# Multiplying w_in by g on two engines instead of three, and storing the remainder rows 64 at a time

## The chip, the core and the metric

The kernel runs on one core of a Trainium2 chip. The metric is the device time of one execution in microseconds; the median of three executions stands for the kernel. The profile is of one further execution, whose own time is given beside its span below. Engine names are those of the profile: PE is TensorE, PEld its weight load, DVE is VectorE, ACT is ScalarE, POOL is GpSimd, SP is SyncE.

## The reference

An attention without softmax, an RMS norm over each head, and a two-layer network with a sigmoid gate, in float32:

```python
# q, k, v: (8, 8, 576, 64); g_norm: (64,); w_in: (512, 2048); w_out: (2048, 512)
kv = np.einsum('bhsd,bhse->bhde', k, v)
out = np.einsum('bhsd,bhde->bhse', q, kv)
rms = np.sqrt(np.mean(out * out, axis=-1, keepdims=True) + 1e-06)
attn_out = out / rms * g_norm
x = attn_out.transpose(0, 2, 1, 3).reshape(B * S, H * D)      # 4608 x 512
h = x @ w_in
g = h * (1.0 / (1.0 + np.exp(-1.702 * h)))
result = g @ w_out                                             # 4608 x 512
```

## The kernel before

**Tiles and passes.** The kernel works in fp16 with float32 sums and has nine passes of the network, `dense(t, ...)`, t = 0 to 8, over 512 rows each. Passes 0 to 7 take the first 512 of the 576 rows of batch t. The 64 rows that each batch has left over are collected in `x_rem` (8 times 64 is 512) and are pass 8. The attention of batch t+1 is woven into pass t as small units that two dictionaries place by hand: `at1(i, f)` runs f after the i-th column block of the first product, `at2(n, f)` after the n-th matmul of the second. The schedule is manual: instructions stand on each engine in the order in which the code emits them, and semaphores are put in where one engine uses what another has made.

**One pass.** The first product (L440) multiplies `w_in_sb`, cut into four blocks `ko` of 128 rows and 2048 columns, by the transposed activations; ScalarE applies the gate (L449) and writes `gT`. The second product (L549), in the class `Seven` (passes 1 to 8), needs seven block products instead of eight, in `ORDER = (1, 5, 6, 2, 7, 3, 4)`, two row blocks `mo` of eight matmuls each, which is 112 matmuls. VectorE forms the sums `gS` (L481) and, from pass 1 on, the sums and copies into the output tile `osb` (L525, L528). In pass 1 the units for batch 2 are: `pack_k` (L227), `kv` (L236, into PSUM; `keep_kv`, L249, copies it to `kvb` in two halves on VectorE), `rows(j)` (L300, four matmuls that need `kvb`, placed at n = 1, 7, 14, 20), their squares on ScalarE (L308), `add_up` (L314), `roots` (L323, L324), `turn` (L327) with a DMA transpose (L333), and `out` for the remainder rows (L279). Pass 2 has the same units.

**w_in times g.** In pass 0 and pass 1 `g_norm` is applied to the activations (L358). From pass 2 on it is in the weights: during the second product of pass 1, which no longer reads `w_in_sb`, `scale_w_in(ko, engine)` multiplies the four blocks, 128x2048 each, in place by the column `g_col` (L206 on ScalarE, L208 on GpSimd or VectorE). Block 0 is on GpSimd at n = 0, block 1 on ScalarE at n = 48, blocks 2 and 3 on VectorE at n = 84 and 96. Pass 2 begins with `mm(ko, fo)` for ko = 0 to 3 on its first column block, so it needs all four within its first four matmuls. On VectorE the scalings stand among `apply` (L362) of the remainder rows of two batches (n = 74 and 80) and the sums L525 into `osb`.

**The last stores.** In pass 8 row block `mo` of `osb` holds the remainder rows of batches 2 mo and 2 mo + 1, 64 partitions each. `place` calls `store_rest` as soon as a quarter is ready: for (1, 1), the right halves of blocks 2 and 3, first; then (0, 1), which completes blocks 0 and 1; then (1, 0), the left halves of blocks 2 and 3. In `out` the rows of one batch's remainder are consecutive for batches from `EARLY` = 2 on; for batches 0 and 1 they are nine rows apart by a step in the index. For blocks with 2 mo >= 2, that is 1, 2 and 3, `store_rest` makes one transfer for both batches, shaped 2 x 64 x columns on the side of `out` and 128 partitions on the side of `osb` (L579); with two queues given it cuts the columns in half. Only block 0 is stored in two transfers of 64 rows (L585), one on SP and one on ScalarE. After the last store SP waits for every transfer to land (L845), and the program ends.

Of the kernel before, what the change touches and what calls it, by code (L numbers as in the profile page):

```python
# [16 lines left out]
def kernel(  # L17
# [10 lines left out]
    nc = tc.nc  # L28

    B, H, S, D = q.shape  # L30
    DM = H * D
# [5 lines left out]
    SM = 512  # L37
    J = SM // P
    R = S - SM
    assert R == 64 and B * R == SM and KO == NPAIR and 2 * D == P  # L40
    NT = B + 1
    EARLY = 2
    PE_ = 96
    NJ = S // PE_
# [36 lines left out]
    HF, HN = FO // 2, DM // 2  # L81
# [61 lines left out]
    for n in "kqv":  # L143
        if n != "q":
            rows = stage.tile([P, H, J * D], F32, name="qf", tag="qf")
            rows = rows.rearrange("p h x -> p (h x)")[0:PE_]
# [8 lines left out]
        out=ident,  # L155
        in_=ident,
# [303 lines left out]
    class Seven:  # L460
# [58 lines left out]
        def place(self, name, mo, with_, i, j):  # L519
            ps, m = self.ready(name, mo)  # L520
            if ps is None:
                return
            o = osbs[self.t][:, 2 * i + m.start : 2 * i + m.stop, j * HN : (j + 1) * HN]
            if with_:
                nc.vector.tensor_add(o, ps, self.kept[with_][:, m])  # L525
            else:
                copy = nc.vector.tensor_copy if self.t == B else nc.scalar.copy
                copy(o, ps)  # L528
            if self.t == B:
                if (i, j) == (1, 0):  # L530
                    store_rest(2 + mo, 0, HN, (nc.sync, nc.scalar))
                elif (i, j) == (1, 1):
                    store_rest(2 + mo, HN, DM, (nc.sync,))
                elif (i, j) == (0, 1):
                    store_rest(0, 0, DM, (nc.sync, nc.scalar))
                    store_rest(1, 0, DM, (nc.sync,))
            elif self.t in HALVED and j == 1 - i:
                store(self.t, 2 * i, 2 * i + 2)

# [31 lines left out]

    def store_rest(mo, n0, n1, queues):
        osb = osbs[B]
        if 2 * mo >= EARLY:
            rows = out.rearrange("(b s) n -> b s n", b=B)[2 * mo : 2 * mo + 2, SM:S, n0:n1]
            half = (n0 + n1) // 2
            parts = [(n0, n1)] if len(queues) == 1 else [(n0, half), (half, n1)]
            for queue, (a, b) in zip(queues, parts):
                queue.dma_start(out=rows[:, :, a - n0 : b - n0], in_=osb[:, mo, a:b])  # L579
            return  # L580
        for g in range(2):
            p0 = SM % PE_
            rows = out[(2 * mo + g) * S : (2 * mo + g + 1) * S, n0:n1]
            rows = rows[bass.DynSlice(NJ * p0 + SM // PE_, R, step=NJ), :]
            queues[g].dma_start(out=rows, in_=osb[g * R : (g + 1) * R, mo, n0:n1])  # L585

    def dense(t, units1, units2, group, deep, hid=None):
# [68 lines left out]
    def store(t, j0, j1):  # L656
        nc.sync.dma_start(
            out=out[t * S : t * S + SM, :].rearrange("(p j) m -> p j m", j=J)[:, j0:j1],
            in_=osbs[t][:, j0:j1],
        )  # L660
# [94 lines left out]
    for t in range(NT):  # L755
        b = t + 1
        u1, u2 = {}, {}

        def at1(i, f, *args):
            u1.setdefault(i, []).append(lambda: f(*args))  # L760

        def at2(i, f, *args):
            u2.setdefault(i, []).append(lambda: f(*args))  # L763

        def of(b, name, *args):
            return lambda: getattr(live[b], name)(*args)

        if t == 0:
            at1(7, of(0, "out", NPAIR))
            at2(4, setattr, a0, "ss_pool", Attention.ss_pool)  # L770
            at2(4, of(0, "ss", NPAIR, True))
            at2(4, of(0, "apply", NPAIR))
            at1(8, start, 1)
            for l in range(2):
                r = slice(l * PH, (l + 1) * PH)
                at1(8, nc.vector.memset, kpad[r, :, :, (1 - l) * D : (2 - l) * D], 0.0)
            for c in range(NPAIR):
                at1(12, of(1, "pack_q", c))
                at2(9 + 3 * c, of(1, "q", c))
                at2((21, 21, 38, 38)[c], of(1, "pack_k", c))  # L780
                at2((36, 37, 46, 47)[c], of(1, "kv", c))
                o = (41, 43, 52, 53)[c]
                at2(o, of(1, "out", c))
                if c == NPAIR - 1:
                    at2(48, load_kv, 2)
                at2((45, 48, 56, 58)[c], of(1, "ss", c))
                at2((48, 51, 56, 60)[c], of(1, "apply", c))
        elif b < B:
            if t == 1:
                at1(5, weight_sums)  # L790
                at2(64, setattr, live[1], "ss_pool", Attention.ss_pool)
                at2(64, of(1, "out", NPAIR))
                at2(80, of(1, "ss", NPAIR))
                at2(80, of(1, "apply", NPAIR))
                at2(0, scale_w_in, 0, nc.gpsimd)
                at2(48, scale_w_in, 1, nc.scalar)
                at2(84, scale_w_in, 2, nc.vector)
                at2(96, scale_w_in, 3, nc.vector)
            f0 = 5 if t == 1 else 2
            at1(f0, cast_q, b)  # L800
            at1(f0, start, b)
            at1(f0, of(b, "transpose_q"))
            if t + 2 < B:
                at1(12 if t == 1 else f0, load_q, t + 2)
                at1((11 if t == 1 else 9) + 4, load_kv, t + 2)
            for c in range(NPAIR):
                at1(f0, of(b, "pack_k", c))
                at1((11 if t == 1 else 9) + c, of(b, "kv", c))
            at2(21, nc.scalar.preload_act_table_set, "natural_log_exp_and_others")
            for j in range(J):  # L810
                at2((1, 7, 14, 20)[j], of(b, "rows", j))
                at2((5, 12, 18, 26)[j], of(b, "add_up", j))
                at2((33, 34, 35, 36)[j], of(b, "turn", j))
            at2(32, of(b, "roots"))
            at2(38, of(b, "out", NPAIR))
            at2(74, of(b, "ss", NPAIR))
            at2(74, of(b, "apply", NPAIR))
            at2(82, nc.scalar.preload_act_table_set, "gelu_apprx_sigmoid_and_others")
        dense(t, u1, u2, (GROUP, 5)[t] if t < 2 else 0, t == 0, None if t else d0)
# [30 lines left out]
```

## Time and profile before

| | us |
|---|---|
| median of three executions | 297.94 (296.08 to 298.21) |
| the profiled execution | 298.24 |
| its span, first to last instruction | 295.8 |

| engine | busy us | share of the span | instructions |
|---|---|---|---|
| PE | 269.0 | 91% | 2136 |
| ACT | 165.5 | 56% | 281 |
| DVE | 161.6 | 55% | 328 |
| POOL | 47.5 | 16% | 74 |

The mean granted clock of TensorE over the span is 0.966. The largest groups are the first product, L440 (512 matmuls with 128x512 outputs, 116.5 us), and the second, L549 (some 900 matmuls with 128x256 outputs). 36.70 MB are read from memory and 9.44 MB written. The profile cuts the span into 40 slices of 7.4 us and gives the busy share of each engine in tenths, the granted clock, and the mean share of the core's 16 DMA engines. Instruction rows are: start in us, duration in us, engine, line, operation, output<-inputs, and in brackets how long the engine had been idle and what released it.

### The profile page before, as it was taken

The numbers are of one execution on the slowest core, as the hardware profiler recorded it, in microseconds if no ns is written. First come the engines' busy times: TensorE is split into PE (matmuls) and PEld (weight loads), VectorE is DVE, ScalarE is ACT, GpSimd is POOL, SyncE is SP. The second block draws the span as 40 slices with busy tenths as digits, with TensorE's granted clock in tenths as the row PEclk, the third lists the DMA queues.
The fourth block names the chain that finished last, engine by engine and source line by source line (L and its number), as shares of the span: only waits on it lengthen the run. The fifth ranks groups of instructions, "written<-read, shape, count | busy, mean of one in ns | idle before, by whom it ended". The sixth has DMA issues, their size and how long they took to land.

```text
span 295.8 us, 5285 instructions
## 1 busy us (share of the span) xinstructions
PE 269.0 (91%) x2136; PEld 175.3 (59%) x2136; DVE 161.6 (55%) x328; ACT 165.5 (56%) x281; POOL 47.5 (16%) x74
## 2 busy tenths in 40 slices
PE   8899999947999999999999999999999999999600
PEld 5444544425864786578558845984697468548500
DVE  2640647996586578476756757684673342052300
ACT  2787258733876665676558475846675751573000
POOL 8852470073001101020111011000000000000000
PEclk9999999995999999999999999999999999999955
DMA  8999999796249957993897499457007000300211
GB/s 175 195 199 206 204 268 222 173 209 127 40 119 180 225 95 196 185 192 71 218 177 152 80 219 240 78 142 152 2 2 212 1 2 0 142 2 1 55 50 36
DMA packets 55400, 38.79 MB, mean 131 GB/s; under 512 B 31152, under 2 KB 52400, under 8 KB 55248
## 3 DMA queue, kind: packets, MB, share of 16 engines
q0 software_dynamic: 16016, 15.55, 33.0%
q1 hardware_dynamic: 39018, 22.65, 31.2%
q8 instruction: 16, 0.26, 0.4%
q10 hardware_dynamic: 342, 0.26, 0.3%
q14 instruction: 8, 0.07, 0.1%
HBM read 36.70 MB, written 9.44 MB: 156 GB/s over the span
## 4 chain that ended last, share of the span: by engine, by line
PE 71%; DMA 12%; DVE 8%; ACT 2%; issue 1%; POOL 0%; DVEq 0%
PE hT L440 33%; PE o L549 32%; DMA w_out_sb<-in_moe_w_out_dram 4%; DMA vbuf<-in_v_dram 4%; DVE gS L481 3%; PE kvp L236 2%; PE outR L300 2%; DMA kraw<-in_k_dram 2%; DMA qraw<-in_q_dram 2%; DVE kpad L227 1%; PE o L618 1%; DVE xT L358 1%; DVE x L327 1%; ACT ln L346 0%; DVE qbuf L136 0%
## 5 line engine op out<-in xcount | busy, mean ns | idle before, releaser
L440 PE MATMUL hT<-xT,w_in_sb 128*128 128x512 f16 x512 | 116.5, 379 | 0.1
L449 ACT ACTIVATE gT<-hT 128x512 f16<-128x512 f32 x144 | 84.5, 601 | 40.7 <-PE hT L440 40.6
L440 PEld LDWEIGHTS <-w_in_sb 128*128 128x128 f16 x576 | 54.5, 98 | 61.1 <-issue 0.6
L549 PEld LDWEIGHTS <-gS 128*128 128x128 f16 x512 | 49.7, 99 | 5.8
L481 DVE TENSOR_TENSOR gS<-gT 128x512 f16<-128x512 f16 (+1 forms) x48 | 24.5, 510 | 45.0 <-ACT gT L449 44.7
L549 PE MATMUL o<-tw,gS 128*128 128x256 f16 x384 | 47.7, 275 | 0.0
L549 PEld LDWEIGHTS <-gT 128*128 128x128 f16 x384 | 37.8, 100 | 6.2
L549 PE MATMUL o<-w_out_sb,gT 128*128 128x256 f16 x256 | 35.1, 281 | 0.0
L227 DVE COPY kpad<-kraw 64x576 f16<-64x576 f16 x56 | 25.0, 446 | 1.3
L525 DVE TENSOR_TENSOR osb<-o,s 128x512 f32<-128x512 f32 (+1 forms) x25 | 16.6, 664 | 15.2 <-issue 9.7
L112 POOL DMA_DIRECT2D kraw<-in_k_dram x16 | 9.9, 622 | 78.3 <-DVE kpad L227 56.9
L308 ACT ACTIVATE sq<-outR 128x512 f16<-128x512 f32 x24 | 14.4, 600 | 12.0 <-PE outR L300 12.0
L314 DVE TENSOR_REDUCE sum<-sq 128x8 f32<-128x512 f16 x24 | 16.4, 684 | 6.4 <-ACT sq L308 6.0
L327 DVE TENSOR_TENSOR x<-outR,sum 128x512 f16<-128x512 f32 x24 | 14.9, 683 | 6.2 <-ACT sum L324 6.2
L517 ACT COPY s<-o 128x512 f32<-128x512 f32 (+1 forms) x26 | 14.3, 550 | 6.5 <-PE o L549 6.4
L618 PE MATMUL o<-w_out_sb,gT 128*128 128x512 f16 x64 | 16.9, 379 | 0.1
L346 ACT ACTIVATE ln<-ss,eps_t 128x512 f32<-128x512 f32 (+1 forms) x16 | 9.3, 582 | 13.4 <-PE ss L344 13.2
L481 DVE TENSOR_TENSOR gS<-gS,gT 128x512 f16<-128x512 f16 (+1 forms) x24 | 16.2, 674 | 0.6
L763 ACT ACT_TABLE_LOAD x12 | 15.4, 1283 | 0.2
L300 PE MATMUL outR<-kvb,qTd 128*128 128x128 f16 x96 | 10.3, 232 | 5.7 <-DVE kvb L249 5.7
L549 PE MATMUL o<-w_out_sb,gS 128*128 128x256 f16 x128 | 15.4, 273 | 0.0
L549 PE MATMUL o<-tw,gT 128*128 128x256 f16 x128 | 15.3, 273 | 0.0
(77 smaller groups left out, 213.3 us busy)
## 6 DMA issues: line engine op xcount, KB each, us to landing
qf<-in_q_dram SPq DMA_DIRECT2D x5, 1024.0 KB
out_dram<-osb SPq DMA_DIRECT2D x10, 512.0 KB
kraw<-in_k_dram POOLq DMA_DIRECT2D x12, 288.0 KB, 7.4
vbuf<-in_v_dram POOLq DMA_DIRECT2D x12, 288.0 KB, 6.9
out_dram<-osb SPq DMA_DIRECT2D x6, 192.0 KB, 4.4
w_in_sb<-in_moe_w_in_dram POOLq DMA_DIRECT2D x4, 256.0 KB, 7.3
w_out_sb<-in_moe_w_out_dram POOLq DMA_DIRECT2D x2, 512.0 KB, 14.8
w_out_sb<-in_moe_w_out_dram POOLq DMA_DIRECT2D x4, 256.0 KB, 10.7
```

The source lines that it names most:

```text
L227: nc.vector.tensor_copy(out=kpad[r, c, :, l * D : (l + 1) * D], in_=kraw[r, c, 0 : NH * D].rearrange("p (j d) -> p j d", j=NH),)
L300: nc.tensor.matmul(t[:, c * P : (c + 1) * P], self.qT[c][:, j * P : (j + 1) * P], self.kb[:, c, :], start=True, stop=True,)
L308: nc.scalar.activation(sq, t, AFT.Square)
L314: nc.vector.tensor_reduce(out=self.sum4[:, j, :], in_=self.o[j][1].rearrange("p (h d) -> p h d", h=H), op=ALU.add, axis=mybir.AxisListType.X,)
L327: nc.vector.tensor_mul(self.x16[:, j, :].rearrange("p (h d) -> p h d", h=H), self.o[j][0].rearrange("p (h d) -> p h d", h=H), self.sum4[:, ...
L440: nc.tensor.matmul(self.h[fo], w_in_sb[:, ko, fo * P : (fo + 1) * P], self.x[:, ko], start=(ko == 0), stop=(ko == KO - 1),)
L449: nc.scalar.activation(self.gT[:, fo, :], self.h[fo], AFT.Gelu_apprx_sigmoid)
L481: op(s[:, n, lo], a, b)
L525: nc.vector.tensor_add(o, ps, self.kept[with_][:, m])
L549: nc.tensor.matmul(o, a, w, start=(p in (1, 2, 5) and i == 0 and (mo == 0 or split)), stop=(i == HF - 1), skip_group_check=True,)
L618: nc.tensor.matmul(os[mo], gT[:, fo, mo * P : (mo + 1) * P], w_out_sb[:, fo, :], start=(fo == 0), stop=(fo == FO - 1),)
L763: u2.setdefault(i, []).append(lambda: f(*args))
```

## The change

Block 0 of `w_in_sb` is multiplied on VectorE at n = 80 and no longer on GpSimd at n = 0; blocks 2 and 3 move from n = 84 and 96 to 92 and 100. Block 1 stays on ScalarE at n = 48. `store_rest` always makes two transfers of 64 rows, one for each batch, with all the columns given; its first queue takes the first batch, its second queue the second. The two calls that gave one queue now give SP twice, or SP and ScalarE.

```diff
                 elif (i, j) == (1, 1):
-                    store_rest(2 + mo, HN, DM, (nc.sync,))
+                    store_rest(2 + mo, HN, DM, (nc.sync, nc.sync))
                 elif (i, j) == (0, 1):
                     store_rest(0, 0, DM, (nc.sync, nc.scalar))
-                    store_rest(1, 0, DM, (nc.sync,))
+                    store_rest(1, 0, DM, (nc.sync, nc.scalar))
...
     def store_rest(mo, n0, n1, queues):
         osb = osbs[B]
-        if 2 * mo >= EARLY:
-            rows = out.rearrange("(b s) n -> b s n", b=B)[2 * mo : 2 * mo + 2, SM:S, n0:n1]
-            half = (n0 + n1) // 2
-            parts = [(n0, n1)] if len(queues) == 1 else [(n0, half), (half, n1)]
-            for queue, (a, b) in zip(queues, parts):
-                queue.dma_start(out=rows[:, :, a - n0 : b - n0], in_=osb[:, mo, a:b])
-            return
         for g in range(2):
-            p0 = SM % PE_
             rows = out[(2 * mo + g) * S : (2 * mo + g + 1) * S, n0:n1]
-            rows = rows[bass.DynSlice(NJ * p0 + SM // PE_, R, step=NJ), :]
+            if 2 * mo + g < EARLY:
+                p0 = SM % PE_
+                rows = rows[bass.DynSlice(NJ * p0 + SM // PE_, R, step=NJ), :]
+            else:
+                rows = rows[SM:S, :]
             queues[g].dma_start(out=rows, in_=osb[g * R : (g + 1) * R, mo, n0:n1])
...
-                at2(0, scale_w_in, 0, nc.gpsimd)
                 at2(48, scale_w_in, 1, nc.scalar)
-                at2(84, scale_w_in, 2, nc.vector)
-                at2(96, scale_w_in, 3, nc.vector)
+                at2(80, scale_w_in, 0, nc.vector)
+                at2(92, scale_w_in, 2, nc.vector)
+                at2(100, scale_w_in, 3, nc.vector)
```

## The prediction

> **What bounds the kernel now.** I read the slices of the page first. PE is at nine tenths or more nearly everywhere, so time can be won only where it is not, or where its clock is low. Two places stand out: the tenth slice (66.6 to 73.9 us), where the clock falls, and the last two, where PE has ended and the DMA engines are almost idle.
>
> ```profile
> span 295.8 us, 5285 instructions
> ...
> PEclk9999999995999999999999999999999999999955
> DMA  8999999796249957993897499457007000300211
> ```
>
> Then the chain of waits through the first place, in order of time (start, length, what), and the instructions behind it:
>
> ```profile
> 61.85 0.19 DVE kvb L249
> ...
> 62.84 4.97 DVE gS L481 x3
> ...
> 67.83 0.28 DVE kvb L249
> ...
> 68.47 0.37 PE outR L300 x2
> ```
>
> ```profile
> 62.38 0.42 DVE L481 TENSOR_TENSOR gS<-gT 128x512 f16<-128x512 f16 x1
> 62.84 4.30 DVE L481 TENSOR_TENSOR gS<-gS,gT 128x512 f16<-128x512 f16 x1
> 63.10 5.48 POOL L208 TENSOR_SCALAR w_in_sb<-w_in_sb,g_col 128x2048 f16<-128x2048 f16 x1
> ...
> 67.83 0.59 DVE L249 CAST kvb<-kvp 64x128 f16<-64x128 f32 x2
> ...
> 68.47 0.26 PE L300 MATMUL outR<-kvb,qTd 128*128 128x128 f16 x1 [5.70 <-DVE kvb L249]
> ```
>
> PE has done half of `rows(0)` and stops for 5.70 us: the other half needs the second copy to `kvb`, which stands on DVE behind the `gS` sums. One of these takes 4.30 us; its neighbours of the same shape take 0.41 or 0.42. What is special beside it is POOL's scaling of block 0. The stretches (length; busy of PE, PEld, DVE, ACT, POOL; granted clock, DMA share, GB/s) show what the stop does afterwards, and the end of the kernel:
>
> ```profile
> 64.16:67.57 3.41, 0.00 (x0) 0.00 (x0) 3.41 (x3) 0.00 (x0) 3.41 (x1) 0.96 1.16 257
> 67.57:70.99 3.42, 2.52 (x16) 1.92 (x16) 2.27 (x6) 1.00 (x2) 1.01 (x1) 0.50 1.12 195
> 70.99:74.39 3.40, 3.40 (x23) 2.68 (x22) 1.37 (x2) 1.45 (x4) 0.39 (x1) 0.54 0.02 4
> ...
> 278.60:282.60 4.00, 0.00 (x0) 0.00 (x0) 0.42 (x1) 0.00 (x0) 0.00 (x0) 0.97 0.44 105
> 282.60:295.80 13.20, 0.00 (x0) 0.00 (x0) 0.00 (x0) 0.00 (x0) 0.00 (x0) 0.50 0.12 41
> ```
>
> PE comes back at half clock and keeps it until about 74.4. At the end the last computation (a copy to `osb`, 278.62, 0.42 us) is over at 279.04, and 16.8 us follow in which a DMA share of 0.12, two engines of sixteen, moves some 43 GB/s. The DMA view from 277 to 296 (40 slices) and SP's issues of L579 there:
>
> ```profile
> DMA  1111628861111111111111111111111111110000
> GB/s 34 28 43 50 71 60 155 194 244 52 37 50 46 20 44 53 44 53 50 47 54 44 53 45 52 50 47 43 43 43 45 43 43 43 43 43 28 0 0 0
> ```
>
> ```profile
> 278.18 9.08 SPq L579 DMA_DIRECT2D out_dram<-osb  x3
> ```
>
> The short burst to 244 GB/s is the pair of 64-row stores (L585, issued at 277.59); the flat rest are the 2 x 64 stores (L579). Even SP's issuing is held up: three issues take 9.08 us.
>
> **POOL's scaling goes.** The blocked sum returns from 4.30 to 0.42 us, so the copies to `kvb` and PE's return come 3.88 us sooner, at 64.59. A stop of 1.82 us stays (62.77 to 64.59): the four sums, 0.35 to 0.46 apart, and two copies still stand ahead. First term: 3.88. On POOL the next instruction (L134 at 72.00) waits for a load in any case, so nothing else moves there.
>
> **The clock.** It fell at about 67.6, 4.8 us after PE stopped; at the end it was still 0.97 on average until 282.6, 3.6 us after the last copy. A stop of 1.8 us is half of the shorter. No row in the middle of the kernel has a stop between 0.63 us (at 79.1, clock 1.00) and 5.70, so the bounds for what is regained are nothing and all; I take all, since both falls came later than 3.5 us. All of it: from the third matmul of `rows(0)` to L279 at n = 38 this pass took 76.01 - 68.47 = 7.54 us, and the next pass, same units at full clock, 105.30 - 100.49 = 4.81. Second term: 2.73. [...]
>
> **Block 0 on DVE.** One scaling there takes 0.74 us and the next instruction follows after 0.66. In times of before, DVE is busy without a gap from 82.57: `apply` at 83.17, scaling at 83.50, sum L525 at 84.16, scaling at 84.76, ended at 85.50, and pass 2 starts at 85.29. After: `apply`, scaling 0 at 83.50, scaling 2 at 84.16, L525 at 84.82, scaling 3 at 85.42, ended at 86.16. Pass 2 needs block 3 in its fourth matmul, at 85.29 + 3 x 0.216 = 85.94, its weights 0.1 earlier. PE waits some 0.35 us, and as PE is the bound this is lost. Bounds: 0 (order has slack) and 0.66 (one whole scaling). Behind it on DVE the casts L136 and packs L227 come 0.66 later; the 2.51 us of idle time before the sums at 93.03 hide that. Without that cover it would cost at most 0.66. The stores L648 on SP (84.87, x8, 4.08 us) wait for L525 and start 0.66 later, and the transpose behind them at 89.06 too; what it delivers is first used at 100.37.
>
> Does everything after this point move with PE? The loads for batch 3 were issued at 59.0 to 62.5, landed by 72.0 and are wanted by pass 2, which would begin at about 79. The transposes of `turn` move from 78.54 to about 71.9, when the DMA share has gone from 1.12 to 0.02. From pass 2 on every load is issued relative to PE's work. So the middle gives 3.88 + 2.73 - 0.35 = 6.26.
>
> **The stores.** SP issues 8 (before 6) and ACT 4 (before 3), all of 64 rows. A 64-row issue takes 0.54 to 0.58 us (L585). SP: blocks 2 and 3, right halves, from 274.77 to about 277.1, hidden before 277.59; then block 0 at 277.59, block 1 at 278.17, left half of 2 at 278.8, of 3 at 279.4 (its data are ready at 279.04); ACT the same beside it. No compute instruction is behind them. From issue to landing, two rows bound the last one: the 32- to 96-row stores L648 of pass 1, 2.6 us; and the L585 pair, whose burst ends at about 281.3, 3.7 us after its issue (its whole landing, 5.8, includes its share on the two crowded engines). The last store is beside others on two queues, as L585 was, but smaller: I take 3.2 in between. SP's last wait ends at 294.9, the program 0.9 later. So 279.4 + 3.2 + 0.9 = 283.5 instead of 295.8: 12.3 us. With 2.6 it is 12.9. The last SP store also reuses the semaphore of a store issued at about 276.6, which may have landed only at 280.3; with that and 3.7 it is 10.9. If landings were no faster than 5.8 us after all, 9.7.
>
> That it is the 2 x 64 shape that binds them to two engines is read from 0.12 against the burst of L585. [...]
>
> **Sum.** 298.24 - 6.26 - 12.3 = 279.7 for the profiled execution; by the median, 0.3 lower.
>
> **Rivals.**
> 1. The clock falls in the shortened stop too. Against it: both falls shown came after 3.6 us or more. 298.24 - 3.53 - 12.3 = 282.4. Chance 0.08.
> 2. The long `gS` sum is not POOL's doing but that of the heavy loads (257 GB/s beside it), and stays. Against it: in pass 2, and while POOL issues loads, the same sum takes 0.42 (98.84). For it: DVE runs on at 67.07 with POOL shown busy until 68.58. Only the stores gain, and the third scaling costs: 298.24 + 0.35 - 12.3 = 286.3. Chance 0.07.
> 3. The stores stay on few engines, because it is the traffic to memory and not the shape that is narrow; only the queue differs. Bytes and pace are the same, three more issues cost up to 1.7 us: 298.24 - 6.26 + 1.7 = 293.7 at worst, 292.0 at best. Against it: the burst at 244 GB/s. Chance 0.06. [...]
> 4. Slower: each 64-row store goes through one engine. The two crowded engines work some 15 us from 279 to 294; on one, this doubles. 298.24 - 6.26 + 15 = 307. It decides from about 6.3 us of added tail, that is, if the mean number of engines falls below 1.4. Against it: the L585 stores have 64 rows and took part in a burst far above two engines' 43 GB/s. Chance 0.03.
>
> The forecast has 0.76. Rivals 1 to 3 are faster by over 1% (3 us, about what a measurement can tell from no change) as well, rival 3 least surely: faster 0.95, same 0.02, slower 0.03. The range takes the forecast's bounds: best 298.24 - 12.9 - 6.61 = 278.7, less about 0.8 for the spread of the runs; worst of its stores 281.1; rival 1, with the worse stores, 283.8. So 277.9 to 283.8.
>
> **What would show it.** After the change: no `gS` sum above 0.7 us; PE's idle time before `rows(0)` 1.8 us instead of 5.7; clock 1.00 from 62 to 74; pass 2 starting about 6.3 us sooner; a wait of PE below 0.7 us there for `w_in_sb`; the span ending some 4 to 5 us after the last copy, with no long stretch at a DMA share of 0.12. The prediction is wrong if the stop stays above 3.5 us, or if the tail stays above 8.

## The result and the profile after

The changed kernel takes 278.56 us (median of four executions, 278.37 to 279.54) against 298.01 us before (median of four as well, 296.08 to 298.21): a ratio of 0.9361, 95% interval 0.932 to 0.9403, as it stands on record; the quotient of the two medians is 0.9347. The profiled execution took 279.54 us with a span of 277.8 us, against 298.24 and 295.8.

The same rows of the page's slices as before. The fall of the clock in the tenth slice is gone, and so are the last slices with an idle PE and a DMA share of one tenth:

```profile
span 277.8 us, 5288 instructions
...
PEclk9999999999999999999999999999999999999999
DMA  8999999979649957991799179917600810030004
```

The instructions around the former stop (start, length, engine, line, what):

```profile
62.72 0.42 DVE L481 TENSOR_TENSOR gS<-gS,gT 128x512 f16<-128x512 f16 x1
...
63.83 0.59 DVE L249 CAST kvb<-kvp 64x128 f16<-64x128 f32 x2
...
64.47 0.27 PE L300 MATMUL outR<-kvb,qTd 128*128 128x128 f16 x2 [1.76 <-DVE kvb L249]
...
69.29 0.28 PE L279 MATMUL outT<-qTr,kvb 128*128 128x64 f16 x4
```

The sum of two inputs at 62.72 takes 0.42 us instead of 4.30, and PE waits 1.76 us instead of 5.70. The stretches that were idle, and then at half clock, before (columns as in the prediction: length; PE, PEld, DVE, ACT, POOL; clock, DMA share, GB/s):

```profile
64.16:67.57 3.41, 3.10 (x36) 2.86 (x36) 2.59 (x6) 2.12 (x4) 0.00 (x0) 1.00 1.16 257
67.57:70.99 3.42, 3.42 (x37) 3.08 (x35) 2.10 (x5) 3.36 (x8) 0.00 (x0) 1.00 1.13 197
```

PE works in them at a granted clock of 1.00. The start of pass 2 shows the price of the third scaling on DVE:

```profile
78.70 1.97 PE L440 MATMUL hT<-xT,w_in_sb 128*128 128x512 f16 x7
78.83 0.74 DVE L208 TENSOR_SCALAR w_in_sb<-w_in_sb,g_col 128x2048 f16<-128x2048 f16 x1
...
79.63 0.76 PEld L440 LDWEIGHTS <-w_in_sb 128*128 128x128 f16 x5 [0.61 <-DVE w_in_sb L208]
```

The load of the next weights idles 0.61 us for block 3, whose scaling ends at 79.57. And the end: the last copy to `osb`, and the DMA view from 270.0 to 277.8 us (40 slices of 0.195 us), with the issues that it lists (size, median time to landing):

```profile
272.60 0.42 DVE L528 COPY osb<-o 128x256 f32<-128x256 f32 x1 [0.45 <-PE o L549]
```

```profile
DMA  7437505710000189998999899998720000000000
GB/s 189 105 89 173 132 5 131 163 32 5 11 16 0 47 200 237 210 189 221 399 326 431 284 336 289 284 305 273 258 79 5 0 0 0 0 0 0 0 0 0
...
out_dram<-osb SPq DMA_DIRECT2D x4, 64.0 KB, 2.7
out_dram<-osb ACTq DMA_DIRECT2D x2, 128.0 KB, 2.7
```

From about 272.7 to 275.5 the DMA share is eight tenths and more, at 190 to 430 GB/s instead of 43. The last copy to `osb` ends at 272.60 + 0.42 = 273.02 us and the span at 277.8, so the tail is 4.8 us instead of 16.8.

So of the 18.0 us by which the span is shorter, 279.04 - 273.02 = 6.0 come from ahead of the last copy and 12.0 from behind it. The profiled execution is 0.7 us shorter besides, outside its span. That part is not the change: time less span, 2.4 us in the profiled execution before and 1.7 in that after, varies between 1.7 and 2.9 us from one execution to the next, with either kernel in much the same way.

### The profile page after: what moved, and what is told of

It reads as the page before. It is cut to its first block, busy times and chain, and to the rows that moved or that the text cites. A ratio compares the mean times of both kernels' runs of the same rounds, so it can differ in the third digit from the quotient of the medians.

```text
span 277.8 us, 5288 instructions
## 1 busy us (share of the span) xinstructions
PE 265.9 (96%) x2136; PEld 173.3 (62%) x2136; DVE 158.1 (57%) x329; ACT 165.4 (60%) x281; POOL 42.1 (15%) x73
## 4 chain that ended last, share of the span: by engine, by line
PE 79%; DVE 8%; DMA 4%; ACT 3%; POOL 2%; issue 1%; DVEq 0%
PE hT L440 39%; PE o L549 30%; PE o L614 4%; DMA vbuf<-in_v_dram 2%; PE kvp L236 2%; PE outR L300 2%; DVE gS L481 1%; DVE kpad L227 1%; DMA xT<-x 1%; POOL qraw L91 1%; ACT ln L346 1%; ACT rs L352 1%; DVE x L327 1%; POOL kraw L91 1%; DVE w_in_sb L208 1%
## 5 line engine op out<-in xcount | busy, mean ns | idle before, releaser
L440 PE MATMUL hT<-xT,w_in_sb 128*128 128x512 f16 x512 | 116.7, 379 | 0.5 <-DMA w_in_sb<-in_moe_w_in_dram 0.3
L449 ACT ACTIVATE gT<-hT 128x512 f16<-128x512 f32 x144 | 84.5, 601 | 41.2 <-PE hT L440 41.2
L440 PEld LDWEIGHTS <-w_in_sb 128*128 128x128 f16 x576 | 54.4, 98 | 62.0 <-DMA w_in_sb<-in_moe_w_in_dram 0.9
L549 PE MATMUL o<-tw,gS 128*128 128x256 f16 x384 | 47.0, 273 | 0.0
L549 PEld LDWEIGHTS <-gT 128*128 128x128 f16 x384 | 37.1, 98 | 5.7
L549 PE MATMUL o<-w_out_sb,gT 128*128 128x256 f16 x256 | 33.5, 273 | 0.0
L112 POOL DMA_DIRECT2D kraw<-in_k_dram x16 | 9.8, 620 | 72.7 <-DVE kpad L227 50.4
L236 PEld LDWEIGHTS <-kpad 128*128 128x128 f16 x252 | 11.1, 98 | 6.4 <-issue 0.2
L112 POOL DMA_DIRECT2D vbuf<-in_v_dram x16 | 9.8, 617 | 32.7 <-PE kvp L236 29.1
```

Source lines behind the costliest of these rows:

```text
L112: nc.gpsimd.dma_start(out=raw[n][l * PH : (l + 1) * PH, c0:c1, 0 : NH * D], in_=srcs[n][b].rearrange("(c l) (p j) d -> l p c (j d)", l=2, ...
L236: nc.tensor.matmul(self.kvp[:, c, :], kpad[:, c, j, :], vbuf[:, c, j * D : (j + 1) * D], start=(j == 0), stop=(j == NH - 1),)
L440: nc.tensor.matmul(self.h[fo], w_in_sb[:, ko, fo * P : (fo + 1) * P], self.x[:, ko], start=(ko == 0), stop=(ko == KO - 1),)
L449: nc.scalar.activation(self.gT[:, fo, :], self.h[fo], AFT.Gelu_apprx_sigmoid)
L549: nc.tensor.matmul(o, a, w, start=(p in (1, 2, 5) and i == 0 and (mo == 0 or split)), stop=(i == HF - 1), skip_group_check=True,)
```

## The experiments

Each experiment was timed beside the kernel before on the same chip; a ratio is to that kernel, with its 95% interval. Four runs separate the parts and test the causes, three look into POOL's block and the clock, and three ask whether what is left over can be had.

**The scaling alone, and the stores alone.** The first has the changed kernel's three `at2` lines and the old `store_rest`; the second has the reverse.

```diff
-                at2(0, scale_w_in, 0, nc.gpsimd)
                 at2(48, scale_w_in, 1, nc.scalar)
-                at2(84, scale_w_in, 2, nc.vector)
-                at2(96, scale_w_in, 3, nc.vector)
+                at2(80, scale_w_in, 0, nc.vector)
+                at2(92, scale_w_in, 2, nc.vector)
+                at2(100, scale_w_in, 3, nc.vector)
```

> The scaling as in the change, the stores as before. My theory: the middle is worth 6.0 us (stop of PE 5.7 to 1.8 us, clock never falls, 0.4 lost at the start of pass 2) and the tail stays 16.8 us: 292.0 us. If the clock's part were not real: 294.7. If the stores did it all: 298.3.

> The stores as in the change, the scaling as before. My theory: the stop of 5.7 us and the half clock stay, the tail falls from 16.8 to 4.8 us: 286.0 us. If the two parts overlapped (a tail shorter only because the middle moved): 290 or more.

Measured: 291.8 us (0.9816, 0.9786 to 0.9846) and 285.02 us (0.9591, 0.9557 to 0.9624), beside 297.87 us before. By the medians that is 6.1 and 12.9 us, together 18.9; by the ratios 5.5 (4.6 to 6.4) and 12.2 (11.2 to 13.2), together 17.7. The interval of the whole change is 17.8 to 20.3 us. So the parts add up as far as these runs can tell, and neither needs the other. The last stretch of the first run, which has the old stores (columns: length; PE, PEld, DVE, ACT, POOL; clock, DMA share, GB/s), still shows the DMA share of 0.12, what two engines of sixteen would give:

```profile
275.50:289.60 14.10, 0.00 (x0) 0.00 (x0) 0.00 (x0) 0.00 (x0) 0.00 (x0) 0.55 0.12 39
```

The second run has POOL's scaling and with it the long sum: 4.49 us, and PE idle for 5.72.

**The stop with a busy PE.** The kernel before, with more matmuls in the stop and nothing else. They write to the half of the bank that the two real matmuls behind them overwrite, so the output is the same.

```diff
             for c in range(NPAIR):
+                if self.b == 2 and j == 0 and c == 2:
+                    for _ in range(36):
+                        nc.tensor.matmul(
+                            t[:, 2 * P : 4 * P],
+                            self.qT[0][:, 0:P],
+                            self.kb[:, 0:2, :].rearrange("p c r -> p (c r)"),
+                            start=True,
+                            stop=True,
+                        )
                 nc.tensor.matmul(
```

> The kernel before, with 36 more matmuls of 0.107 us on PE in its stop, into a bank that is overwritten afterwards; DVE and POOL do as before. My theory: the stop still ends at about 68.5 us, but the clock doesn't fall and the 2.7 us after the stop are regained: 295.3 us. Rival (the slow stretch after the stop comes from ScalarE, VectorE or the loads): 298.0.

Measured: 295.48 us (0.9916, 0.9886 to 0.9945; 1.6 to 3.4 us faster). PE and DVE there, and the stretch that was at half clock before:

```profile
62.23 4.09 PE L302 MATMUL outR<-kvb,qTd 128*128 128x256 f16 x36
68.12 0.27 PE L309 MATMUL outR<-kvb,qTd 128*128 128x128 f16 x2 [1.79 <-DVE kvb L249]
...
72.93 0.28 PE L279 MATMUL outT<-qTr,kvb 128*128 128x64 f16 x4
```

```profile
62.30 4.49 DVE L490 TENSOR_TENSOR gS<-gS,gT 128x512 f16<-128x512 f16 x1
```

```profile
67.57:70.99 3.42, 2.87 (x34) 2.65 (x34) 2.59 (x7) 1.89 (x4) 0.66 (x1) 1.00 0.94 159
```

The long sum is there and the real work resumes as late as before, at 68.12. But the clock is 1.00 in all four stretches from 62.77 to 74.39, and from 68.12 to L279 it takes 4.81 us, not 7.54. More work on PE made the kernel faster, so the slow stretch behind the stop was the clock, and neither the loads nor the other engines.

**All stores on SP.** The changed kernel, with `(nc.sync, nc.sync)` at all four calls of `store_rest`.

> The changed kernel with all twelve 64-row stores on SP. My theory (the shape decides how many DMA engines work): eight issues of 0.6 us in a row after 271.6, the last at 275.8 instead of 274.0, so 280.3 us. Rival (the second queue is what helps): the tail goes back to 14 us or more, 288 or above.

Measured: 281.78 us (0.9485, 0.9436 to 0.9533). SP's twelve issues and the time to landing:

```profile
268.94 8.44 SPq L581 DMA_DIRECT2D out_dram<-osb  x12
```

```profile
DMA to landing us min/median/max: 2.0/2.4/3.4
```

The stores land as fast as with two queues (2.0, 2.7 and 3.4 there). By the medians the kernel takes 3.2 us more than the changed one. In the traces the tail is 2.1 us longer, 6.9 against 4.8, and this part is issue; what makes up the rest is not shown. The eight behind the last computations begin at 272.36, not 271.7, since SP's fourth store took 1.46 us to issue, and follow each other every 0.63 us, so the last is issued at 276.8. I expected 1.7 us more; the mechanism is the expected one, its price was too low. What shrank the tail, from 16.8 us before to 6.9 with one queue, is the shape of the transfers, 64 rows each and not 2 x 64. That the shape decides how many engines work is read from the DMA share, 0.12 before and up to nine tenths here; no run shows how many engines one transfer had. That there are more transfers comes with the shape, and no run has one without the other. The second queue is worth 2 to 3 of its 12 us.

**What of POOL's work blocks DVE.** The changed kernel with POOL busy at the old place, on a tile of its own, and DVE's scalings as in the change. First a multiplication in place, as before but on other data; then, in its stead, three memsets, which only write. Both runs fill the tile once while the kernel loads.

```diff
+    scratch = const.tile([P, DFF], F16)
...
+    nc.gpsimd.memset(scratch, 1.0)
...
+                at2(0, nc.gpsimd.tensor_scalar_mul, scratch, scratch, g_col)
```

```diff
+                for _ in range(3):
+                    at2(0, nc.gpsimd.memset, scratch, 1.0)
```

> The changed kernel with one more operation on POOL at the old place: a tile of 128x2048 that nothing else uses is multiplied by g_col in place (block 0 stays on VectorE). My theory (POOL's access to SBUF blocks the gS sum, whatever data it works on): the sum of 0.42 us takes over 4 us again, PE stops for 5.6 us, the clock falls, about 285 us. Rival (the sum waited for w_in_sb or for the loads): 278.6, sum 0.42.

> As the last, but POOL only writes there (three memsets of that tile) and reads nothing. If only POOL's reads stand in the way of a sum with two inputs from SBUF: sums at 0.42 us, 278.6 us. If any POOL access does: one sum over 1 us, PE's stop longer by as much.

Measured, one execution each: 284.92 and 278.33 us. DVE and POOL in the first run:

```profile
62.66 4.46 DVE L482 TENSOR_TENSOR gS<-gS,gT 128x512 f16<-128x512 f16 x1
...
63.10 5.46 POOL L761 TENSOR_SCALAR scratch<-scratch,g_col 128x2048 f16<-128x2048 f16 x1
```

and in the second:

```profile
62.47 1.83 POOL L761 MEMSET scratch<- 128x2048 f16 x1
62.74 0.42 DVE L482 TENSOR_TENSOR gS<-gT,gS 128x512 f16<-128x512 f16 x1
...
63.80 0.43 DVE L482 TENSOR_TENSOR gS<-gT 128x512 f16<-128x512 f16 x1
```

The block needs neither `w_in_sb` nor its dependencies: the same multiplication on a tile that nobody else touches lengthens the sum to 4.46 us, stops PE for 5.7 and halves the clock from 65.9 to 72.7 us. With POOL writing for 5.6 us (three memsets of 1.8) and reading nothing, every sum beside it takes 0.42 to 0.43. So it is not POOL's being busy that stands in the way of the sum (4.46 us beside the multiplication, 0.42 beside the memsets). The multiplication reads its tile and the memsets read nothing, so these two runs point to POOL's reading; that another difference between the two operations does it, they don't rule out. Whether an operation of DVE with one input would be held too, no run shows: only this sum stands beside POOL's multiplication while it holds. By the records the sum begins first (62.66 us, and POOL's multiplication at 63.10), and yet the sum is the one that is held. The records of POOL may be offset, however; see the last section.

**Half a block, for the clock.** The changed kernel with half of block 0's columns on POOL, for a stop of PE between 1.8 and 5.7 us.

```diff
-    def scale_w_in(ko, engine):
-        w = w_in_sb[:, ko]
+    def scale_w_in(ko, engine, f0=0, f1=DFF):
+        w = w_in_sb[:, ko, f0:f1]
...
-                at2(80, scale_w_in, 0, nc.vector)
+                at2(0, scale_w_in, 0, nc.gpsimd, 0, DFF // 2)
+                at2(80, scale_w_in, 0, nc.vector, DFF // 2, DFF)
```

> The changed kernel with half of block 0 (128x1024) on POOL at the old place, the other half on VectorE at n = 80. My theory: a block of half the length, some 2 us more on the sum, PE's stop 3.6 to 3.8 us. [...]

Measured: 280.47 us, one execution.

```profile
62.48 1.87 DVE L481 TENSOR_TENSOR gS<-gS,gT 128x512 f16<-128x512 f16 x1
...
62.92 2.88 POOL L208 TENSOR_SCALAR w_in_sb<-w_in_sb,g_col 128x1024 f16<-128x1024 f16 x1
```

```profile
PE outR L300 <- DVE kvb L249: 3.1, 1, 3.1
```

The sum is 1.45 us longer than without POOL, not 2, so the stop is 3.1 us and not 3.6 to 3.8, and the run says nothing on stops of that length. The clock stays at 1.00 behind it. So a stop of 3.1 us left the clock alone in this one execution, where one of 5.7 halves it. It is no bound: at the end of the same trace PE's last matmul is over at 273.23 us, and the clock is halved from 275.3 on, 2.1 us later.

**What is left over.** Three runs on one chip: the changed kernel again; block 0 on DVE at n = 66, in a gap, with blocks 2 and 3 at their old places; and the same with the first stores on two queues.

```diff
-                at2(80, scale_w_in, 0, nc.vector)
-                at2(92, scale_w_in, 2, nc.vector)
-                at2(100, scale_w_in, 3, nc.vector)
+                at2(66, scale_w_in, 0, nc.vector)
+                at2(84, scale_w_in, 2, nc.vector)
+                at2(96, scale_w_in, 3, nc.vector)
```

```diff
-                    store_rest(2 + mo, HN, DM, (nc.sync, nc.sync))
+                    store_rest(2 + mo, HN, DM, (nc.sync, nc.scalar))
```

> The changed kernel as it is, measured on the same chip as the next two so that they can be compared with it: 278.6 us by every theory.

> The changed kernel with block 0 scaled on VectorE at n = 66 instead of 80 (in a gap of 1.93 us there, while VectorE waits for ScalarE), blocks 2 and 3 at 84 and 96 as before the change. My theory: PE's wait for w_in_sb at the start of pass 2 (0.6 us for its weights, 0.4 us lost) goes, and nothing else is late: 0.4 us faster than the changed kernel, 278.2. Rival (another wait takes its place, such as the activations of pass 2): no change.

> As the last, and the first four stores (right halves of blocks 2 and 3) on SP and ScalarE instead of SP alone. My theory: SP was held up by its fourth store (1.39 us) and its last began 0.95 us after its data were ready; without that the last store starts some 0.6 us sooner: 277.6 us. Rival (the last landing depends on how many stores are in flight, not on SP's issue): 278.2.

| | us, median of six | ratio to before, interval |
|---|---|---|
| changed kernel | 279.2 (278.57 to 279.91) | 0.9385 (0.9356 to 0.9414) |
| block 0 earlier | 278.94 (278.32 to 279.18) | 0.9375 (0.9349 to 0.9401) |
| and the first stores on two queues | 278.45 (278.06 to 280.5) | 0.9372 (0.934 to 0.9404) |

The intervals overlap nearly wholly, so no version is shown to be faster than another. In the traces the first aim was met: with block 0 earlier the wait for `w_in_sb` at the start of pass 2 is gone, and from there to the last copy it takes 272.15 - 78.41 = 193.74 us, against 273.02 - 78.70 = 194.32 in the changed kernel. Of this 0.58 us the wait is 0.3; the rest is another one (see below). The second aim is not shown: the last store is issued 0.68 us after the last copy instead of 1.00, but in the second trace of the changed kernel, without this edit, it is 0.68 as well.

That a few tenths don't show in the medians is no wonder, since the start of the kernel varies by more. Pass 2 began at 78.41 us in the trace with block 0 earlier and at 80.08 in that with the first stores on two queues. The first matmul of L440 waits longer for a load in the latter, and behind this wait the clock is low in the third slice, from 13.98 to 17.40 us:

```profile
PE hT L440 <- DMA w_in_sb<-in_moe_w_in_dram: 1.2, 1, 1.2
```

```profile
PEclk9979999999999999999999999999999999999998
```

This matmul starts 0.4 us later than in the other trace (13.81 against 13.40), and the low clock costs 1.3: from this matmul to the second of L344 behind it the kernel takes 18.16 - 13.81 = 4.35 us, and 16.45 - 13.40 = 3.05 there.

## Why the prediction was right

**POOL's scaling.** The prediction put the sum back from 4.30 to 0.42 us and PE's stop at 1.82 us; the trace has 0.42 and 1.76. Its rival, that the long sum was due to the loads, falls by the two POOL runs: the loads are the same in both (a DMA share of 1.11 and 1.13 from 62 to 64 us), and only the run in which POOL reads has a long sum, 4.46 us against 0.42.

**The clock.** Predicted 2.73 us regained, from 7.54 to 4.81 us between the third matmul of `rows(0)` and L279. In the trace it is 69.29 - 64.47 = 4.82. The run with a busy PE isolates it: 1.6 to 3.4 us. The outcome is well borne out: in all seven traces in which PE stops here for 1.3 to 1.8 us the clock stays at 1.00. The reason given for it is not. The prediction read two falls of the clock in coarse stretches and took the shorter delay, 3.6 us, for a bound with room to spare (in finer stretches the falls are 4.5 us, at 67.3, and 3.75 us, at 282.3, after PE's last matmul). In the experiments the clock fell 2.0 us after PE's last matmul (at the end with block 0 earlier), 2.1 (half a block), and 3.1 (in the stop of the run in which POOL reads), while at the end of the changed kernel it had not fallen after 5.2. And at the start of the last version it halved for 3.4 us after a longest stop of only 1.16 us, in a stretch (10.57 to 13.98 us) in which PE was busy for 1.97 of 3.41 us. So the length of a stop alone does not decide. The rival in which a shorter stop lowers the clock too does occur in this kernel, at another place; that the place of the change is safe is shown by the seven traces and not by the prediction's margin.

**Block 0 on DVE.** The order and the times on DVE came out to the hundredth: 6.59 us earlier, as pass 2 is, scaling 3 was put at 85.42 to 86.16 and ran from 78.83 to 79.57. Its price was put at 0.35 us and is 0.3: the first gate of pass 2 (L449) begins 80.06 - 78.70 = 1.36 us after its first matmul, against 86.35 - 85.29 = 1.06 before, and in four other traces with the same three scalings on DVE (the scaling alone, one queue, the two POOL runs) the time from the start of pass 2 to the last copy is 194.0 us, against 279.04 - 85.29 = 193.75 before. In the changed kernel's two traces it is 194.32 and 194.28, since the start of a later pass waits a second time, for a transpose:

```profile
PEld L440 <- DMA xT<-x: 0.4, 1, 0.4
```

This wait, at 220.30, costs the other 0.27 us. It is in neither the kernel before nor those four runs, so it isn't the price of the scaling; why the transpose was late there stays open. The prediction, in which all that follows moves with PE, has no term for it. The cover for the casts and packs behind the third scaling held: until that wait the gates of every pass keep the distance of 0.3.

**The stores.** Predicted: last issue 279.4 (273.4, when shifted by the 6.0 us won ahead of it), 3.2 us to landing, 0.9 to the end; in all 12.3 us won. Measured: last issue 274.02, 2.5 to landing by the trace's landing events, 1.3 to the end; 12.0 won. The issue was late since SP's fourth store took 1.39 us, where no store of 32 to 96 rows before had taken over 0.69; the landing was a little faster than the better of the two bounds, that of the 32- to 96-row stores of pass 1 (2.6); the end took 0.4 more. The three errors nearly cancel, which is luck. In the second trace of the same kernel no store of SP took over 0.59 us, and the tail is 277.17 - 272.71 = 4.5 us, as forecast (283.5 - 279.04). The rival of a narrow path to memory falls by the run with one queue, whose stores still reach a median of 2.4 us to landing, and by the flat 0.12 of the run with the old shapes; the slower rival, one engine for each 64-row store, by the 190 to 430 GB/s.

**Sum.** 6.26 and 12.3 were forecast, 6.0 and 12.0 came, in the span. 279.7 was forecast for the profiled execution, which took 279.54; this is closer than the terms are, by luck, since the time outside the span was 0.7 us shorter in this execution and the sum had held it constant. By the median 279.4 was forecast and 278.56 came.

## What to carry to other kernels

An operation on an engine that looks idle isn't free if it lengthens one on the path, as POOL's multiplication did here: look at the neighbours' durations, where one of several equal instructions takes ten times as long (4.30 us, and 0.41 or 0.42). A stop of PE of some microseconds can have a second price, the slower clock after it (2.7 us here, after a stop of 5.70), so that filling it with useless matmuls can already help (1.6 to 3.4 us here). Don't take one measured delay until the clock falls for a bound: here it was between 2.0 and over 5.2 us, and once the clock halved with no stop over 1.16 us ahead of it. For the last transfers of a kernel look at the DMA share behind the last computation: here it was 0.12, what two engines of sixteen would give, and the remedy was transfers of 64 rows each and not of 2 x 64, worth 9 to 10 of the 12 us, at least three times the second queue.

## What the runs showed of the hardware that was not expected

**POOL's record and the delay of the sum are offset.** The sum began ahead of POOL's record in each run, by 0.26 us (before), 0.44 (multiplication on its own tile) and 0.44 (half a block), although it needs only 0.42, and was held all the same. And in each it ended 1.44 or 1.45 us before POOL's record does: 67.14 and 68.58, 67.12 and 68.56, 64.35 and 65.80. So the sum was delayed by 1.4 to 1.6 us less than POOL's record is long (3.88 of 5.48 before, 1.45 of 2.88 for the half block), and later sums ran at 0.41 while POOL was still shown as busy. It looks as if POOL's record were later than its reading; no run shows that directly.

**SP's fourth issue in a row.** In the changed kernel the first three of SP's 64 KB stores took 0.54 to 0.58 us to issue and the fourth 1.39. It is so in five of the eight traces with four such stores in a row on SP (1.28 to 1.53 us), and not in the three others, among them the second trace of the very same kernel, where none took over 0.59. So it belongs to the execution and not to the code alone. What holds the fourth was not tried.
